# The start of a fused FFT and expert kernel: folds of a tile in one chain, classes of tiles by turns

## The chip, the cores and the metric

The kernel runs on one core of one Trainium2 chip. The time is device microseconds from launch to end; lower is better. Before the change three runs took 2414.26, 1863.13 and 1863.0 us, the median is 1863.13.

## The reference, cut to what matters

```python
batch, seq, dim = (8, 3008, 256)
X = np.fft.fft(x, axis=1)
X = np.fft.fft(X, axis=2)
x = X.real.astype(np.float32).reshape(B * S, D)     # (24064, 256)
h = x @ w_in                                         # w_in (256, 2048)
r = np.maximum(h, 0.0)
out = ((r * r) @ w_out).astype(np.float32)           # w_out (2048, 256)
```

The weights arrive as 64-bit floats, the activations as 32-bit ones.

## The kernel before, in words

The Fourier transform along the sequence is taken as products with cosine and sine tables, and its length is cut by symmetry before TensorE sees it. A batch is loaded as rows of four: n, -n, M-n and M+n (S is the length of the sequence, M half of it). A **fold** adds and subtracts these four and then the columns d and D-d. It leaves a tile `w` whose first 129 columns are for the cosine part, called P, and whose other 128 are for the sine part, called Q. The transform along the second axis is folded into the weights: a **window** of `w_in` is multiplied by cosine and sine matrices of size 256 (`dft_win`, L351), and the results are kept as G1 and G2 (`keep_win`). The **front** of a block is then G1 times P plus or minus G2 times Q, and relu and square follow; the **back** multiplies by `w_out`.

For batch 0 the rows are cut into seven tiles, by class: tile 0 (95 rows) and tile 1 (94 rows) of the classes 0 and 1, tiles 2 and 3 (96 and 92 rows) of class 2, called `TWO`, tiles 4 to 6 (128, 128 and 120 rows) of class 3, called `ODD0` onwards. Each class has its own cosine table; the sine table of tile 0 is loaded, the others are made by ScalarE from the cosine tables (`turn_table`, L228). A product group is named by its part and tile: P4 is the cosine product of tile 4, Q4 its sine product, E4 a small extra product for the sine part's lone column, which ScalarE scales out of `w` (L575) into `lone`. Each name stands for two products, for even and odd frequencies (`kp`). Products (L758) gather in PSUM; ScalarE copies the first quarter out (`copy`, L777), VectorE joins the groups step by step (`join_4`, `join_2`, `lo`; L799 to L811), and the odd group of each part is kept (`keep`, L818) for a later `rest` and `hi`.

The **head** is everything up to `sp` (`spread_e`, L983), which spreads the last row of Qt over all partitions, so that front half steps of block 0 (L999, L1001) can begin. The order of the head is written out by hand, and each engine takes its instructions in the order of the program. Six of seven tiles are folded in two halves on VectorE: the P half is `fs` (L554), `sc` (L563), `w` (L572, two steps), the Q half is `fd` (L559), `sc` (L567), `w` (two steps). Each step needs the one before it. The Q half of tile 5 is folded by GpSimd (`q_beside`, L1308 to L1312). All P halves but two come ahead of most Q halves. TensorE runs filler products on the identity matrix (`awake`, L255): 34 at the start, 5 before the first window, 2 before Q's joins; a filler is two matmul instructions in the trace, as is every product on 32-bit numbers.

Weights are converted from 64-bit to 32-bit numbers by a `round`: VectorE takes the signs (L300, phase TS), ScalarE scales the upper half and the lower half (L305 and L310, PU and PL), VectorE shifts and joins (L320, H), GpSimd adds the two (L329, PR). Windows 0 and 1 are begun in the head; the others, and the eight of `w_out`, run between the steps of block 0.

Loads go through SP's queue, those of the small tables through GpSimd's. Tiles 0 to 3 lie in the buffers that later hold `g`, tiles 4 to 6 and most raw weights in three buffers, and a raw weight's load waits until its buffer's last reader is done. For window 0 the last row of G2 is written to DRAM and read back by SP's queue as a column (`take_ends`); the windows named in `BY_PRODUCTS` get it by two products of one column (`ends_of`, L367) and a copy by VectorE (`keep_ends`, L371).

Behind the head stands `ORDER`, a list of tokens for block 0: `f0a` is TensorE's first half of front 0, `d0a` VectorE's half step for it (L1014 to L1017), `pgC1` and `pgD1` are the products of window 1 with the cosine and sine matrices, `GC1` and `GD1` keep them, `fe1` and `gE1` are its end products and their copy, `rl` and `sq` are relu and square, `bk` is a back step (L1122). After it comes the loop over all other blocks: L1028 is the front there, L1093 the back, on sums that GpSimd makes (L1056 to L1073).

Of the kernel before, what the change touches and what calls it, by code (L numbers as in the profile page):

```python
# [15 lines left out]
P = 128  # L16
# [68 lines left out]
def kernel(  # L85
# [84 lines left out]
    def load_x(b, t):  # L170
        if b and (t >= ODD0 or t == TWO + 1):
            xt[b, t] = xp.tile([P, 4, D], F32, name="xt", tag="x")
            for p, first, count, step in later_rows(t):
                nc.sync.dma_start(out=xt[b, t][p:p + count], in_=x[b, first:first + step * (count - 1) + 1:step])
            return
        c, r0, step, rows = TILES[t]

        while rows % 15 and rows % 16 and r0 + step * rows < NROW:
            rows += 1

        pool, tag = (gp, "g") if b == 0 and t < NT - NX else (xp, "x")
        xt[b, t] = pool.tile([P, 4, D], F32, name="xt", tag=tag)
        nc.sync.dma_start(out=xt[b, t][0:rows], in_=x[b, r0:r0 + step * (rows - 1) + 1:step])
# [68 lines left out]
    def awake(n):  # L252
        filled = psh.tile([P, CH], F32, name="filled", tag="h")
        for _ in range(n):
            nc.tensor.matmul(filled[:, 0:P], ident, ident, start=True, stop=True)  # L255
# [90 lines left out]
    def dft_win(j, side):  # L346

        tab, nm = ((cosd, "mC"), (sind, "mD"))[side]
        pg = psm.tile([P, CH], F32, name="pg", tag=nm) if j else psh.tile([P, CH], F32, name="pg", tag="h")
        for i in range(2):  # L350
            nc.tensor.matmul(pg, tab[:, i], win[j][:, i], start=i == 0, stop=i == 1)  # L351
        return pg

    BY_PRODUCTS = (1, 2)

    def keep_win(j, side, pg):
        to, v = (G1, G2)[side].rearrange("p (h j f) -> j p h f", h=2, j=NJ)[j], pg.rearrange("p (h f) -> p h f", h=2)
# [177 lines left out]
    def next_sums():  # L535
        nonlocal folds
        folds += 1
        return sums[folds % 2]

    def next_halves():  # L540
        nonlocal turns
        turns += 1
        return halved[turns % 2]

    def fold(t):


        r = slice(0, TILES[t][3])
        st = states[t] = {}
        folded[0, t] = w = wp.tile([P, 2, D + 1], F32, name="w", tag="w")  # L550

        def f_s():
            st["fs"], v = next_sums(), xt[0, t]
            tt(out=st["fs"][r, :, 0:D], in0=v[r, 0::2], in1=v[r, 1::2], op=ADD)  # L554

        def f_d():
            st["fd"] = fp.tile([P, 2, D], F32, name="fd", tag="fd")
            v = xt[0, t]
            tt(out=st["fd"][r], in0=v[r, 0::3], in1=v[r, 1:3], op=SUB)  # L559

        def f_sc():
            st["sc"], s = next_halves(), st["fs"]
            tt(out=st["sc"][r, :, PART[0]], in0=s[r, :, 0:H + 1], in1=s[r, :, D:H - 1:-1], op=ADD)  # L563

        def f_dc():
            st["sc"], d = next_halves(), st["fd"]
            tt(out=st["sc"][r, :, PART[1]], in0=d[r, :, 1:H + 1], in1=d[r, :, D - 1:H - 1:-1], op=SUB)  # L567

        def f_w(part):
            v = st["sc"]  # L570
            for kp in range(2):
                tt(out=w[r, kp, part], in0=v[r, 0, part], in1=v[r, 1, part], op=SUB if kp else ADD)  # L572

        def f_e():
            nc.scalar.mul(lone[r, 2 * t:2 * t + 2, P - 1:], w[r, :, H:H + 1], -0.5 if TILES[t][0] else 0.5)  # L575

        return [f_s, f_d, f_sc, f_dc, lambda: (f_w(PART[0]), f_e()), lambda: f_w(PART[1])]

    def by(i, a):
        return turn[0:HALF2, a, i:i + 1]  # L580
# [707 lines left out]

    pieces = [fold(t) for t in range(NT)]
    (_, start), *groups = dft_ops(0)
    groups = dict(groups)

    def for_p(t):
        for i in (0, 2, 4):
            pieces[t][i]()

    def for_q(t):
        for i in (1, 3, 5):  # L1300
            pieces[t][i]()

    def q_beside(t, behind):


        r, v = slice(0, TILES[t][3]), xt[0, t]
        gt, d = nc.gpsimd.tensor_tensor, states[behind]["sc"]
        gt(out=d[r, :, 0:D], in0=v[r, 0::3], in1=v[r, 1:3], op=ALU.subtract)  # L1308
        sc = next_halves()
        gt(out=sc[r, :, PART[1]], in0=d[r, :, 1:H + 1], in1=d[r, :, D - 1:H - 1:-1], op=ALU.subtract)  # L1310
        for kp in range(2):
            gt(out=folded[0, t][r, kp, PART[1]], in0=sc[r, 0, PART[1]], in1=sc[r, 1, PART[1]],  # L1312
               op=ALU.subtract if kp else ALU.add)

    def p_part(*names):
        for nm in names:
# [5 lines left out]
            for kp in range(2):  # L1322
                groups[1, kp, nm]()

    def folds_of(names):
        for nm in names.split():
            (for_p if nm[0] == "P" else for_q)(int(nm[1:]))

    def products_of(names):
        for nm in names.split():  # L1330
            (p_part if nm[0] == "P" else q_part)({"P": "", "Q": "", "E": "e"}[nm[0]] + nm[1:])

    start()
    awake(34)
    load_x(0, 0)
    load_x(0, 1)
    load_table(cosT, cos_s, (0,))
    nc.scalar.copy(turn[0:1, 0, 0:1], ident[0:1, 0:1])
    nc.gpsimd.tensor_copy(turn[0:1, 0, 1:2], xt[0, 0][0:1, 0, 0:1])
    load_table(cosT, cos_s, (1, TWO, TWO + 1), nc.gpsimd)  # L1340
    folds_of("P0 Q0 P1 Q1")
    raw = {("in", 0): load(pair_in(0))}
    first = round_win(0, raw["in", 0])
    first[0]()
    first[1]()
    load_x(0, 2)
    load_x(0, 3)
    for dst, src in ((cosd, cos_d), (sind[:, :, 0:P - 1], sin_d)):
        nc.sync.dma_start(out=dst, in_=src.rearrange("(c p) m -> p c m", p=P))
    load_table(sinT, sin_s, (0,), nc.gpsimd)  # L1350
    load_x(0, ODD0)
    load_x(0, ODD0 + 1)
    load_table(cosT, cos_s, (ODD0,))
    load_x(0, ODD0 + 2)
    load_table(cosT, cos_s, (ODD0 + 1, ODD0 + 2))
    for j in (1, 2):
        raw["in", j] = load(pair_in(j))
    folds_of("P2")
    first[2]()
    first[3]()  # L1360
    products_of("P0 E0 P1 E1")
    awake(5)
    for a in range(2):
        keep_win(0, a, dft_win(0, a))
    take_ends(0)
    folds_of("P3")
    products_of("P2 P3")
    p_part("copy")
    products_of("E2 E3")
    for t in range(1, ODD0):  # L1370
        turn_table(t)
    folds_of("P4 P5 Q2 P6 Q3 Q4")
    products_of("P4 Q0 Q1 E4 Q2 P5 P6")
    for t in range(ODD0, NT):
        turn_table(t)
    products_of("E5 Q3 E6 Q4")
    q_beside(5, 4)
    for nm in ("join_4", "join_2", "lo"):
        groups[0, 0, nm]()
    for nm in ("join_4", "join_2", "lo"):  # L1380
        groups[0, 1, nm]()
    p_part("keep")
    q_part("copy")
    products_of("Q5")
    second = round_win(1, raw["in", 1])
    second[0]()
    second[1]()
    folds_of("Q6")
    products_of("Q6")
    awake(2)  # L1390
    for nm in ("join_4", "join_2"):
        groups[1, 0, nm]()
    second[2]()
    second[3]()
    for nm in ("join_4", "join_2"):
        groups[1, 1, nm]()
# [48 lines left out]
    def piece_beside():  # L1445
# [7 lines left out]
    ROUNDED = ['3', 'w0', '4', 'w1', '5', 'w2', '6', 'w3', '7', 'w4', 'w5', 'w6', 'w7']  # L1453
    PHASES = ('TS', 'PW', 'H', 'PR', 'PU', 'PL')
    ORDER = (
# [8 lines left out]
    ).split()  # L1464
    rounds = {"2": round_win(2, raw["in", 2])}
    loaded, freed = [], set()
    made = {}

# [260 lines left out]
```

## Time and profile before

| | us |
|---|---|
| median of three runs | 1863.13 |
| the profiled execution | 1862.73 |
| its span, first to last instruction | 1860.9 |
| TensorE waits in the whole span, the seven kinds named added up | 4.4 |
| VectorE starts its first fold | 4.50 |
| TensorE starts its first product on data | 11.43 |
| the spread of Qt's last row (L983) | 34.13 |
| first back step of block 0 (L1122) | 47.76 |
| first front of the loop (L1028) | 91.42 |

The page gives busy times of each engine over the span. PE is TensorE's matmul, PEld its weight load, DVE is VectorE, ACT ScalarE, POOL GpSimd, SP the queue that issues most loads. Start times in a timeline are microseconds from the first instruction. An instruction's row ends with what ended the idle time ahead of it, where there was any. A row can hold several equal instructions (x2), and then its second number is the time from the first start to the last end. Two steps on VectorE that don't depend on each other overlap by some hundredths of a microsecond, so that the distance from start to start is a little shorter than the duration of a row.

### The profile page before, as it was taken

To read this page: it belongs to the slowest core of one execution; us is meant where nothing else is said; L and a number is where in the kernel's file an instruction comes from. 1 tells how busy PE (TensorE), PEld (TensorE's weight loads), DVE (VectorE), ACT (ScalarE), POOL (GpSimd) and SP (SyncE) were. 2 spreads that over 40 slices of the span, in tenths; PEclk is the share of its full clock that TensorE was granted. 3 is DMA by queue.
4 is the path that set the end of the run, shared out by engine and by line. 5 is a ranking of instruction groups with operands and counts; after the bars stand their busy time and mean duration, and the time that the engine had idled before them with its cause. 6 is when DMAs were issued, how large, how long until landed. Compare 5 with 4: busy or idle time off the path is not lost.

```text
span 1860.9 us, 33983 instructions
## 1 busy us (share of the span) xinstructions
PE 1852.5 (100%) x11368; PEld 1750.9 (94%) x11368; DVE 1475.5 (79%) x3483; ACT 1075.1 (58%) x1592; POOL 1461.7 (79%) x2137
## 2 busy tenths in 40 slices
PE   9999999999999999999999999999999999999999
PEld 7699999999999999999999999999999999999998
DVE  8998878887788878888788787888877887757666
ACT  4776646565556655666456565566645666444454
POOL 4499778788788887888778887788877878788885
PEclk9999999999999999999999999999999999999999
DMA  7441001110011111111011100111001100000010
GB/s 204 115 61 40 19 21 54 41 29 23 21 43 42 29 22 32 32 46 31 15 32 46 48 16 15 45 46 35 15 21 42 38 15 21 17 21 15 21 43 23
DMA packets 153541, 69.52 MB, mean 37 GB/s; under 512 B 132851, under 2 KB 144601, under 8 KB 153368
## 3 DMA queue, kind: packets, MB, share of 16 engines
q1 hardware_dynamic: 152822, 66.80, 14.5%
q8 instruction: 91, 1.49, 0.3%
q14 instruction: 82, 0.67, 0.1%
q0 software_dynamic: 416, 0.43, 0.1%
q10 hardware_dynamic: 130, 0.12, 0.0%
HBM read 42.60 MB, written 24.69 MB: 36 GB/s over the span
## 4 chain that ended last, share of the span: by engine, by line
PE 94%; DVE 3%; POOL 2%; ACT 1%; DMA 0%; issue 0%; SPq 0%; DVEq 0%; POOLq 0%; ACTq 0%
PE F L1093 34%; PE S L1093 23%; PE hQ L1028 17%; PE hP L1028 17%; PE pd L881 1%; PE pd L855 1%; PE pd L758 1%; DVE fd L320 1%; PE fin L1202 0%; DVE he L1014 0%; DVE w L572 0%; DVE wsum L404 0%; PE pg L351 0%; DVE g L1017 0%; DVE fs L554 0%
## 5 line engine op out<-in xcount | busy, mean ns | idle before, releaser
L1041 ACT ACTIVATE g<-g 128x1008 f32<-128x1008 f32 (+1 forms) x384 | 399.4, 1040 | 306.0 <-DVE g L1037 282.5
L1032 DVE SCALAR_TENSOR_TENSOR he<-ew,gE,hP 128x252 f32<-128x252 f32 (+1 forms) x748 | 321.3, 471 | 284.9 <-PE hP L1028 284.9
L1044 ACT ACTIVATE g<-g 128x1008 f32<-128x1008 f32 (+1 forms) x384 | 399.4, 1040 | 12.0
L1028 PE MATMUL hQ<-Qt,G 128*128 128x252 f32 (+3 forms) x1496 | 379.3, 376 | 0.6 <-ACT g L1041 0.5
L1028 PE MATMUL hP<-Pt,G 128*128 128x252 f32 (+1 forms) x1496 | 378.8, 376 | 0.0
L1093 PE MATMUL F<-s,wsum 128*128 128x168 f32 (+1 forms) x1496 | 335.4, 306 | 0.0
L1028 PEld LDWEIGHTS hQ<-Qt,G 128*128 128x128 f32 (+1 forms) x1496 | 281.6, 190 | 38.5 <-issue 2.6
L1093 PE MATMUL F<-g,wout 128*128 128x168 f32 (+1 forms) x1496 | 304.1, 305 | 0.0
L1066 POOL TENSOR_TENSOR s<-g 128x168 f32<-128x168 f32 (+1 forms) x187 | 100.8, 539 | 253.8 <-ACT g L1044 129.1
L1036 DVE TENSOR_TENSOR g<-he,hQ 128x504 f32<-128x504 f32 (+1 forms) x374 | 253.0, 676 | 41.0 <-DVE he L1032 1.8
L1028 PEld LDWEIGHTS hP<-Pt,G 128*128 128x128 f32 x1496 | 266.0, 190 | 18.7 <-issue 0.7
L1093 PE MATMUL S<-s,wout 128*128 128x168 f32 (+1 forms) x1496 | 280.6, 306 | 0.8 <-POOL s L1073 0.8
L1093 PE MATMUL F<-g,wsum 128*128 128x168 f32 (+1 forms) x1496 | 273.5, 305 | 0.0
L1093 PE MATMUL S<-s,wsum 128*128 128x168 f32 (+1 forms) x1496 | 273.5, 305 | 0.0
L1037 DVE TENSOR_TENSOR g<-he,hQ 128x504 f32<-128x504 f32 (+1 forms) x374 | 251.0, 671 | 0.0
L1093 PEld LDWEIGHTS F<-s,wsum 128*128 128x128 f32 x1496 | 247.6, 190 | 0.0
L1093 PEld LDWEIGHTS F<-g,wsum 128*128 128x128 f32 x1496 | 239.3, 190 | 8.1
L1093 PEld LDWEIGHTS S<-s,wsum 128*128 128x128 f32 x1496 | 239.3, 190 | 8.1
L1093 PEld LDWEIGHTS F<-g,wout 128*128 128x128 f32 x1496 | 239.4, 190 | 0.0
L1093 PEld LDWEIGHTS S<-s,wout 128*128 128x128 f32 x1496 | 231.0, 190 | 1.7 <-POOL s L1073 1.0
L1069 POOL TENSOR_TENSOR s<-s 128x336 f32<-128x336 f32 (+1 forms) x187 | 168.4, 901 | 14.7
L1072 POOL TENSOR_TENSOR s<-s 128x336 f32<-128x336 f32 (+1 forms) x187 | 167.7, 897 | 14.7
(221 smaller groups left out, 2484.3 us busy)
## 6 DMA issues: line engine op xcount, KB each, us to landing
out_dram<-os SPq DMA_DIRECT2D x376, 56.0 KB
xt<-in_x_dram SPq DMA_DIRECT2D x39, 384.0 KB
xt<-in_x_dram SPq DMA_DIRECT2D x63, 128.0 KB
raw<-in_moe_w_out_dram SPq DMA_DIRECT2D x20, 256.0 KB
ew<-e_dram SPq DMA_DIRECT2D x39, 126.0 KB
out_dram<-os SPq DMA_DIRECT2D x288, 7.0 KB
raw<-in_moe_w_in_dram SPq DMA_DIRECT2D x16, 256.0 KB
xt<-in_x_dram SPq DMA_DIRECT2D x2, 512.0 KB
```

The source lines that it names most:

```text
L320: nc.vector.scalar_tensor_tensor(out=e, in0=high, scalar=3, in1=e, op0=ALU.logical_shift_left, op1=ALU.bitwise_or)
L758: nc.tensor.matmul(ps[0:w.shape[-1]], w, part_of(cosT if lone_e else tab, t)[0:rows, kp, PLACE[t]:PLACE[t] + NC[kp][c]], start=t == ts[0] ...
L1028: nc.tensor.matmul(to[:, h, 0:n], w[:, fs], v[:, ks], start=h == 0, stop=True, skip_group_check=True)
L1032: nc.vector.scalar_tensor_tensor(out=t[:, h, 0:n], in0=window[b, k0][:, 0:n], scalar=gE[:, fc:fc + 1], in1=hP[:, h, 0:n], op0=ALU.mult, op ...
L1036: tt(out=g[:, :, 0:n], in0=t[:, :, 0:n], in1=hQ[:, :, 0:n], op=ALU.add)
L1037: tt(out=g[:, :, n:2 * n][:, :, ::-1], in0=t[:, :, 0:n], in1=hQ[:, :, 0:n], op=ALU.subtract)
L1041: act(g[:, :, 0:2 * n], g[:, :, 0:2 * n], AF.Relu)
L1044: act(g[:, :, 0:2 * n], g[:, :, 0:2 * n], AF.Square)
L1066: gt(out=s[:, 11], in0=b2[:, 0], in1=b1[:, 0], op=SUB)
L1069: gt(out=s[:, 4:6], in0=s[:, 4:6], in1=s[:, 10:11].to_broadcast([P, 2, tb]), op=SUB)
L1072: gt(out=s[:, 6:9:2], in0=s[:, 2:4], in1=s[:, 6:8], op=ADD)
L1093: nc.tensor.matmul(acc[nm][:, slot, 0:tb], w, v, start=q == 0 and nm not in begun, stop=q == end - 1, skip_group_check=True)
```

## The change

- A tile is folded in one go: both wide steps (sum and difference), both half steps, then `w` for P and Q together in two steps of 257 columns. GpSimd folds nothing.
- The tiles are taken by turns of the classes: 0, 4, 1, 5, 2, 3, 6. Each is followed by all its products P, E and Q. The loads and the tables stand in that order; tile 0's sine table is now the first load of GpSimd's queue, and window 0's raw block comes behind tile 2.
- Of the fillers 24 stand at the start and 7 behind P0 and E0; the others go.
- P's joins are set between the folds and the last products, Q's behind Q6. Window 0's products come between E6 and Q6, into another PSUM pool.
- Window 0's last row goes by end products and a copy in the head, no longer through DRAM.
- Window 1's step H (L320) and its GpSimd product move from the head to the start of `ORDER`, behind `sp`. In `ORDER` front half 0b moves ahead of window 1's products, and step H of window 2 goes behind `d0a`.

```diff
-    BY_PRODUCTS = (1, 2)
+    BY_PRODUCTS = (0, 1, 2)
...
+        fs, sc = next_sums(), next_halves()
+        fd = fp.tile([P, 2, D], F32, name="fd", tag="fd")
+        tt(out=fs[r, :, 0:D], in0=v[r, 0::2], in1=v[r, 1::2], op=ADD)
+        tt(out=fd[r], in0=v[r, 0::3], in1=v[r, 1:3], op=SUB)
+        tt(out=sc[r, :, PART[0]], in0=fs[r, :, 0:H + 1], in1=fs[r, :, D:H - 1:-1], op=ADD)
+        tt(out=sc[r, :, PART[1]], in0=fd[r, :, 1:H + 1], in1=fd[r, :, D - 1:H - 1:-1], op=SUB)
+        for kp in range(2):
+            tt(out=w[r, kp], in0=sc[r, 0], in1=sc[r, 1], op=SUB if kp else ADD)
...
     start()
-    awake(34)
+    awake(24)
...
+    fold(0)
+    products_of("P0 E0")
+    awake(7)
+    turn_table(ODD0)
+    fold(ODD0)
+    products_of("P4 E4 Q0")
+    products_of("Q4")
+    turn_table(1)
+    fold(1)
+    for j in (1, 2):
+        raw["in", j] = load(pair_in(j))
+    products_of("P1 E1 Q1")
+    p_part("copy")
+    turn_table(ODD0 + 1)
+    fold(ODD0 + 1)
+    p_part("join_4")
+    q_part("copy")
+    products_of("P5 E5 Q5")
     first[0]()
     first[1]()
...
+    turn_table(TWO)
+    fold(TWO)
+    products_of("P2 E2 Q2")
     first[2]()
     first[3]()
...
+    turn_table(TWO + 1)
+    fold(TWO + 1)
+    products_of("P3 E3 Q3")
+    turn_table(ODD0 + 2)
+    fold(ODD0 + 2)
+    products_of("P6 E6")
     second = round_win(1, raw["in", 1])
     second[0]()
     second[1]()
...
+    p_part("join_2")
+    for a in (1, 0):
+        keep_win(0, a, dft_win(0, a))
     products_of("Q6")
...
+    ends = ends_of(0)
+    q_part("join_4", "join_2")
+    p_part("lo", "keep")
+    keep_ends(0, ends)
     q_part("lo")
...
-        'sp TS2 PU2 f0a et PL2 TS3 H2 pgD1 PR2 d0a pgC1 f0b GC1 PW3 d0b pgC2 GD1 TSw0 rl0 fe1 f1b lc4 H3 PWw0 f1a gE1 PR3 '
+        'sp H1 PR1 TS2 PU2 TS3 f0a et PL2 f0b PW3 d0a H2 PR2 pgD1 d0b pgC1 GD1 TSw0 GC1 lc4 H3 PR3 rl0 PWw0 fe1 f1b gE1 pgC2 f1a '
```

More of the change, by code (lines that the diff above doesn't have):

```diff
@@ L348, in dft_win @@
         tab, nm = ((cosd, "mC"), (sind, "mD"))[side]
-        pg = psm.tile([P, CH], F32, name="pg", tag=nm) if j else psh.tile([P, CH], F32, name="pg", tag="h")
+        pg = psm.tile([P, CH], F32, name="pg", tag=nm) if j else psd.tile([P, CH], F32, name="pg", tag="d")
         for i in range(2):
@@ L545, in fold @@
     def fold(t):
-        r = slice(0, TILES[t][3])
-        st = states[t] = {}
+        r, v = slice(0, TILES[t][3]), xt[0, t]
         folded[0, t] = w = wp.tile([P, 2, D + 1], F32, name="w", tag="w")
[L552 to L577, printed above, removed]
+        fs, sc = next_sums(), next_halves()
[6 more added lines that the diff above has]
+            tt(out=w[r, kp], in0=sc[r, 0], in1=sc[r, 1], op=SUB if kp else ADD)
+        nc.scalar.mul(lone[r, 2 * t:2 * t + 2, P - 1:], w[r, :, H:H + 1], -0.5 if TILES[t][0] else 0.5)
     def by(i, a):
@@ L1287, in ahead @@
         return one + two
-    pieces = [fold(t) for t in range(NT)]
     (_, start), *groups = dft_ops(0)
     groups = dict(groups)
[L1295 to L1313, printed above, removed]
     def p_part(*names):
@@ L1323, in q_part @@
                 groups[1, kp, nm]()
-    def folds_of(names):
-        for nm in names.split():
-            (for_p if nm[0] == "P" else for_q)(int(nm[1:]))
     def products_of(names):
@@ L1333 @@
     start()
-    awake(34)
+    awake(24)
     load_x(0, 0)
+    load_table(cosT, cos_s, (0,))
+    load_x(0, ODD0)
     load_x(0, 1)
-    load_table(cosT, cos_s, (0,))
     nc.scalar.copy(turn[0:1, 0, 0:1], ident[0:1, 0:1])
     nc.gpsimd.tensor_copy(turn[0:1, 0, 1:2], xt[0, 0][0:1, 0, 0:1])
+    load_table(sinT, sin_s, (0,), nc.gpsimd)
     load_table(cosT, cos_s, (1, TWO, TWO + 1), nc.gpsimd)
-    folds_of("P0 Q0 P1 Q1")
+    load_table(cosT, cos_s, (ODD0,))
+    load_x(0, ODD0 + 1)
+    load_table(cosT, cos_s, (ODD0 + 1,))
@@ L1342 @@
+    load_x(0, TWO)
     raw = {("in", 0): load(pair_in(0))}
-    first = round_win(0, raw["in", 0])
+    load_x(0, TWO + 1)
+    for dst, src in ((cosd, cos_d), (sind[:, :, 0:P - 1], sin_d)):
+        nc.sync.dma_start(out=dst, in_=src.rearrange("(c p) m -> p c m", p=P))
+    load_x(0, ODD0 + 2)
+    load_table(cosT, cos_s, (ODD0 + 2,))
+    first = round_win(0, raw["in", 0])
+    fold(0)
[4 more added lines that the diff above has]
+    products_of("P4 E4 Q0")
@@ L1344 @@
+    products_of("Q4")
[10 more added lines that the diff above has]
+    products_of("P5 E5 Q5")
     first[0]()
     first[1]()
[L1346 to L1358, printed above, removed]
+    turn_table(TWO)
+    fold(TWO)
+    products_of("P2 E2 Q2")
     first[2]()
     first[3]()
[L1361 to L1383, printed above, removed]
@@ L1384 @@
-    products_of("Q5")
+    turn_table(TWO + 1)
[4 more added lines that the diff above has]
+    products_of("P6 E6")
     second = round_win(1, raw["in", 1])
@@ L1387 @@
     second[1]()
-    folds_of("Q6")
+    p_part("join_2")
+    for a in (1, 0):
+        keep_win(0, a, dft_win(0, a))
     products_of("Q6")
[L1390 to L1396, printed above, removed]
+    ends = ends_of(0)
+    q_part("join_4", "join_2")
+    p_part("lo", "keep")
+    keep_ends(0, ends)
     q_part("lo")
@@ L1464 @@
     ).split()
-    rounds = {"2": round_win(2, raw["in", 2])}
+    rounds = {"1": second, "2": round_win(2, raw["in", 2])}
     loaded, freed = [], set()
```

## The prediction, as put on record before the run

> **What bounds the kernel now.** I read the page's busy times first, then who waited for whom on TensorE, then the stages of the start in a table by stretches, then the timelines of TensorE, VectorE and GpSimd over the first 40 us.
>
> From the page, engine totals:
>
> ```profile
> PE 1852.5 (100%) x11368; PEld 1750.9 (94%) x11368; DVE 1475.5 (79%) x3483; ACT 1075.1 (58%) x1592; POOL 1461.7 (79%) x2137
> ```
>
> TensorE's waits over the whole span (two of seven rows; the longest is 1.4 us at the first instruction):
>
> ```profile
> PE pg L351 <- POOL win L329: 0.8, 1, 0.8
> PE S L1093 <- POOL s L1073: 0.8, 1, 0.8
> ```
>
> The stretches (length, then PE, PEld, DVE, ACT, POOL busy):
>
> ```profile
> 11.40:34.10 22.70, 21.73 (x108) 16.55 (x106) 21.80 (x63) 10.65 (x29) 6.85 (x8) 1.00 0.89 258
> 34.10:45.80 11.70, 11.38 (x54) 9.49 (x55) 9.31 (x25) 8.73 (x17) 3.68 (x3) 1.00 0.36 75
> 45.80:91.40 45.60, 45.60 (x153) 28.58 (x152) 42.61 (x92) 34.49 (x55) 19.69 (x16) 1.00 0.48 121
> ```
>
> TensorE has next to no hole after 45.8 us, so the end comes as much earlier as the dense stretch begins earlier. What matters is when the head ends: the spread of Qt's last row (L983) at 34.13. In the head the bound is VectorE: 21.80 busy of 22.70, and its row stretches from 4.50 to 34.07 without a wait. TensorE's rows there hold filler and products that start late:
>
> ```profile
> 1.37 10.22 PE L255 MATMUL filled<-ident 128*128 128x128 f32 x68 [1.37 <-POOL ident masks.py:199]
> 11.43 0.58 PE L758 MATMUL pd<-cosT,w 95*128 95x95 f32 x4
> 13.25 1.31 PE L255 MATMUL filled<-ident 128*128 128x128 f32 x10
> 19.77 1.43 PE L758 MATMUL pd<-cosT,w 128*128 128x377 f32 x4
> 33.34 0.61 PE L255 MATMUL filled<-ident 128*128 128x128 f32 x4
> 34.13 0.69 PE L983 MATMUL pe<-Qt,ident 128*128 128x252 f32 x2 [0.18 <-DVE Qt L737]
> ```
>
> VectorE, whose rows price a fold, and GpSimd beside it:
>
> ```profile
> 12.91 0.68 DVE L320 SCALAR_TENSOR_TENSOR fd<-raw,fd 128x512 uint32<-128x512 uint32 x1
> 13.52 0.68 DVE L554 TENSOR_TENSOR fs<-xt 92x512 f32<-92x512 f32 x1
> 14.23 1.37 DVE L563 TENSOR_TENSOR sc<-fs 92x258 f32<-92x258 f32 x1
> 16.77 0.43 DVE L563 TENSOR_TENSOR sc<-fs 128x258 f32<-128x258 f32 x1
> 17.23 0.49 DVE L572 TENSOR_TENSOR w<-sc 128x129 f32<-128x129 f32 x2
> 28.57 0.89 DVE L559 TENSOR_TENSOR fd<-xt 120x512 f32<-120x512 f32 x1
> 33.47 0.60 DVE L799 SCALAR_TENSOR_TENSOR Qt<-pd,signs,w 128x126 f32<-128x126 f32 x2
> 36.29 0.42 DVE L1016 TENSOR_TENSOR g<-he,ph 128x252 f32<-128x252 f32 x1
> ```
> ```profile
> 13.75 1.57 POOL L329 TENSOR_TENSOR win<-fd,m 128x512 int32<-128x512 int32 x1 [1.08 <-DVE fd L320]
> 25.82 1.30 POOL L1308 TENSOR_TENSOR sc<-xt 128x512 f32<-128x512 f32 x1 [10.50 <-DVE w L572]
> 36.15 1.27 POOL L329 TENSOR_TENSOR win<-fd,m 128x512 int32<-128x512 int32 x1 [2.40 <-ACT m L310]
> ```
>
> The sum of a tile took 1.37 us where 0.43 is usual, beside GpSimd's product of window 0. The step at 36.29 lies beside such a product too and is not lengthened; one of its inputs is in PSUM.
>
> **The folds.** A P half costs 1.59 us on VectorE (fs rows at 16.05 and 17.64), a Q half the same (24.07 to 25.66), each a chain in which every step waits for the one before. The new chain has its two wide steps side by side: 0.61 us each (12.91 to 13.52 is the spacing of two such rows without a dependence), 0.34 for the first half step (36.29 to 36.63 for the row's successor), 0.46 for the second up to its user (16.77 to 17.23), and twice 0.34 for w over all 257 columns in place of four steps: 2.7 us against 3.18. For seven tiles that is 18.9 us; before, 13 halves took 20.7 on VectorE, and the 14th 3.1 on GpSimd (25.82 to 28.92). VectorE so gains 1.8 us and takes back what GpSimd did.
>
> **The head, added up.** Tile 0 lands as before: VectorE starts at 4.50. Four folds (0, 4, 1, 5) end at 15.3. The order of loads follows them: by the DMA rates of the stretches (223 GB/s in the first 10 us, 285 in the next) the 0.99 MB up to tile 4 are through by about 6, the need is at 7.2; tile 5's 2.3 MB, with up to 0.4 MB of tables from GpSimd's queue, by 10.2 to 11.7, need 12.6. Nothing is charged; if tile 5 were 1 us late, 1 us is added. P's first joins then wait for TensorE: 24 fillers at 0.296 (10.05 us for 34) end at 8.5, P0 E0 take 0.9, 7 fillers at 0.26 end at 11.2; P4 E4 2.5 (0.63 a product of 377 columns), Q0 0.4, Q4 1.3, P1 E1 0.85: 16.2 with the copy of the first group under the second. So VectorE stands 0.9 us, and four joins at 0.16 end at 16.9. Window 0's raw block is now behind tile 2: 3.6 to 4.0 MB, that is 14.8 to 17.2; it is its L300 that waits, with the folds of 2, 3 and 6 queued behind it. I take no wait, since the joins end at 16.9; 0.3 is the bound. L300 0.35, fold 2 to 19.95, L320 to 20.55. GpSimd's product of window 0 now falls beside fold 3, as it fell beside the step at 14.23: I charge 0.95, that row's excess (bounds 0 and 1.57, the whole product). Fold 3 ends at 24.2, and fold 6's first w is there at 26.65. Tile 6 and its table, 5.2 to 5.5 MB in all, are through by 20.5 to 22.5 (210 GB/s from 20 on), window 1's raw block by 24.5, each 2 us or more ahead of its user; the cover gone, each us late is one us.
>
> From here TensorE leads: P6 E6 2.5, window 0 (L351) 1.7, Q6 1.3, the new end products of window 0 0.4 (the row at 43.64 up to the next, 44.01): 32.5. VectorE has its L300 (0.35), P's joins (four at 0.27, rows 26.10 and 26.37), Q's (2.4, 30.44 to 33.47 less one L320) and P lo (0.4) done at 31.1, so they are covered with 1.3 us to spare. Then the copy into gE with its wait 0.3, Qt's two joins 0.6, spread at 33.4: **0.7 us earlier** than 34.13.
>
> **What is moved past the head.** Window 1's L320 (0.61) and its GpSimd product (1.27) now come behind the spread; VectorE's two L300 and the first half step of block 0 queue behind that L320. Ahead of L351 of window 1 TensorE has the spread 0.43 and now both halves of front 0, 1.7. The product is ready 0.05 before the spread plus 0.69, 1.27 and up to 0.42 for an L300 in its way: 2.0 to 2.4 against 2.1. I charge 0.3. In 34.1 to 45.8 VectorE idles 2.4 us, which hides the 0.61; without that idle it would be 0.61. The write and read of window 0's last row through DRAM go: they held SP's queue, so raw blocks 3, w0, 4 and w1 start earlier; by the table DMA has room (75 GB/s), a gain I count at nothing, as none of VectorE's waits names a raw block. ScalarE has the same table turns, spread out; it is busy 10.65 of 22.70.
>
> Sum: 0.7 less 0.3, that is 0.4 earlier. The profiled execution took 1862.73 (span 1860.9), so 1862.3; the median of the runs is 0.4 above it: **1862.7**.
>
> [...]
>
> **The rivals.**
> *The cover holds:* no step is held beside GpSimd, and window 1 comes in time: 0.95 and 0.3 more, 1861.4. For it: a new fold has its wide steps back to back, and GpSimd may find its place between. Against: the row at 14.23. 0.2.
> *GpSimd holds VectorE behind the spread (slower):* L300 and L320 have only SBUF inputs, and two windows' products come there at once. Such rows cost 1.77 and 2.01 in place of 0.69 at 55.16 and 57.20 beside GpSimd's 55.08 and 57.08, that is 1.1 and 1.3 more. If both hit before TensorE is dense, block 0's half steps and the next windows come 2.4 later and no hole later on gives it back: 1862.7 + 2.4 = 1865.1. It decides when the holds exceed the 2.4 us that VectorE idles there, or fall on the two window products. [...] No row shows two windows at the spread: 0.25.
> *It leads nowhere:* the head ends earlier, but raw blocks or GpSimd's sums (100.0 busy of 108.6 in 91.4 to 200) set the next stage: 1863.1. Against: both follow from the same head, and TensorE waited on them 0.8 us once. 0.1.
>
> **How the numbers follow.** Forecast 0.45, rivals 0.2, 0.25, 0.1. Downwards the cover's 1861.4 less the 0.9 of P's joins, if TensorE comes sooner, is 1860.5; upwards 1865.1, with the 1 us of a late tile 1866.1. Leaving out under a tenth at each end: 1860.8 to 1865.8. A measurement of this kernel tells about 2% from no change, 37 us; the whole head is 34 us and no case reaches it: within 2% 0.97, faster 0.01, slower 0.02.
>
> **What would show it.** Folds of 2.7 us; one VectorE step of fold 3 lengthened beside window 0's product; P6 behind 26.6; the spread near 33.4; L351 of window 1 waiting no more than 0.4 for GpSimd; L1028's first row, 91.42 before, near 91.0. Wrong if VectorE waits for a load between 4.5 and 27, if Q6's products start after 31.5, or if TensorE's holes between the spread and the first plain product (L1122) grow.

## The result, and the profile after

Twenty runs of the kernel after took 1866.64 us in the median (1863.32 to 1869.21), beside 1863.05 for the kernel before on the same chip (all but one run of it between 1862.71 and 1863.96): ratio 1.0018, 95% interval 1.0011 to 1.0024. The forecast was 1862.7, its range ended at 1865.8. The kernel became slower by 3.6 us, and its time, which hardly moved before, now scatters over 6 us. The profiled execution took 1864.92 (span 1863.1, before 1860.9), 2.2 more than the profiled one of before but 1.7 less than the median.

The page's totals of the kernel after:

```profile
PE 1852.8 (99%) x11352; PEld 1749.8 (94%) x11352; DVE 1475.5 (79%) x3474; ACT 1074.8 (58%) x1592; POOL 1458.6 (78%) x2133
```

The same three stretches as before. Columns: length, busy time of PE, PEld, DVE, ACT, POOL with instruction counts, granted TensorE clock, DMA share, GB/s:

```profile
11.40:34.10 22.70, 20.71 (x85) 14.84 (x85) 19.30 (x50) 9.26 (x27) 2.77 (x3) 0.92 1.01 269
34.10:45.80 11.70, 10.79 (x54) 8.85 (x53) 10.49 (x27) 8.03 (x17) 3.87 (x3) 1.00 0.24 46
45.80:91.40 45.60, 45.60 (x157) 29.31 (x156) 42.56 (x93) 34.51 (x57) 20.50 (x15) 1.00 0.48 123
```

Two columns of the first row matter. VectorE is busy 19.30 of 22.70 where it was busy 21.80, 2.5 us less, in part because Qt's joins and window 1's L320 now lie behind 34.1; it stands idle for 3.4 us. The granted clock is 0.92 where it was 1.00.

TensorE's timeline. The lines of the program have moved: L739 is a product, L964 the spread:

```profile
8.99 0.58 PE L739 MATMUL pd<-cosT,w 95*128 95x95 f32 x4
11.45 1.43 PE L739 MATMUL pd<-cosT,w 128*128 128x377 f32 x4
22.41 0.80 PE L739 MATMUL pd<-sinT,w 96*127 96x189 f32 x4
25.14 0.92 PE L739 MATMUL pd<-cosTl,w 92*128 92x189 f32 x4 [1.92 <-DVE w L557]
27.90 2.43 PE L739 MATMUL pd<-cosTl,w 120*128 120x377 f32 x4
30.16 1.43 PE L739 MATMUL pd<-cosTl,wsum 120*128 120x377 f32 x4
33.16 1.43 PE L739 MATMUL pd<-sinTl,w 120*127 120x377 f32 x4
35.78 0.66 PE L964 MATMUL pe<-Qt,ident 128*128 128x252 f32 x2 [0.86 <-DVE Qt L718]
```

Products start at 8.99 in place of 11.43, but the spread comes at 35.78 in place of 34.13. TensorE stands 1.92 us ahead of P3 until fold 3's `w` is there. P6, at 27.90, takes 2.43 us; E6 behind it, of the same shape, takes 1.43. The clock tells why. The same columns, in three stretches of 3.41 us laid on the step of the granted clock:

```profile
23.00:26.41 3.41, 1.49 (x10) 1.24 (x9) 3.38 (x7) 0.34 (x2) 0.40 (x1) 1.00 1.09 290
26.41:29.82 3.41, 3.41 (x9) 2.37 (x8) 3.38 (x12) 2.50 (x5) 0.00 (x0) 0.50 1.05 381
29.82:33.23 3.41, 3.41 (x15) 2.53 (x14) 2.22 (x9) 0.38 (x1) 0.00 (x0) 1.00 0.84 266
```

Behind the stretch in which TensorE worked 1.49 of 3.41 us the granted clock was 0.50 for one stretch of that length, and then 1.00 again.

VectorE's timeline, where the folds' lateness comes from (L552 to L557 are the steps of a fold, L300 and L320 those of a raw block):

```profile
7.96 0.69 DVE L552 TENSOR_TENSOR fs<-xt 128x512 f32<-128x512 f32 x1 [0.88 <-DMA xt<-in_x_dram]
16.44 0.25 DVE L786 TENSOR_TENSOR db<-da,pd 128x95 f32<-128x95 f32 x1 [0.37 <-ACT da L758]
17.98 0.43 DVE L300 TENSOR_SCALAR fd<-raw 128x512 uint32<-128x512 uint32 x1 [0.80 <-DMA raw<-in_moe_w_in_dram]
22.20 1.75 DVE L553 TENSOR_TENSOR fd<-xt 92x512 f32<-92x512 f32 x1
25.34 0.68 DVE L552 TENSOR_TENSOR fs<-xt 120x512 f32<-120x512 f32 x1
34.97 0.16 DVE L371 COPY gE<-pe 128x2 f32<-128x2 f32 x1 [2.93 <-PE pe L367]
36.17 1.84 DVE L300 TENSOR_SCALAR fd<-raw 128x512 uint32<-128x512 uint32 x2
```

GpSimd, whose products lie beside the lengthened rows at 22.20 and 36.17:

```profile
21.84 1.56 POOL L329 TENSOR_TENSOR win<-fd,m 128x512 int32<-128x512 int32 x1 [8.87 <-DVE fd L320]
36.40 1.33 POOL L329 TENSOR_TENSOR win<-fd,m 128x512 int32<-128x512 int32 x1 [13.00 <-DVE fd L320]
```

VectorE waits for tile 4 of x (0.88), for P's copy (0.37) and for window 0's raw block (0.80), and one wide step of fold 3 takes 1.75 in place of 0.68; fold 6 starts at 25.34. Behind the spread nothing is lost: the first back step is at 49.23, 13.45 us behind the spread, where it was 13.63. In the loop another 0.6 us is added in this execution: the first fronts stand 1.50 behind those of before, the ones from 739 us on 2.13.

### The profile page after: what moved, and what is told of

Its sections match the earlier page's. It is cut to its first block, busy times and chain, and to the rows that moved or that the text cites. A ratio compares the mean times of both kernels' runs of the same rounds, so it can differ in the third digit from the quotient of the medians.

```text
span 1863.1 us, 33926 instructions
## 1 busy us (share of the span) xinstructions
PE 1852.8 (99%) x11352; PEld 1749.8 (94%) x11352; DVE 1475.5 (79%) x3474; ACT 1074.8 (58%) x1592; POOL 1458.6 (78%) x2133
## 3 DMA queue, kind: packets, MB, share of 16 engines
q8 instruction: 91, 1.49, 0.3%
## 4 chain that ended last, share of the span: by engine, by line
PE 94%; DVE 2%; POOL 1%; ACT 0%; issue 0%; DMA 0%; SPq 0%; DVEq 0%; POOLq 0%; ACTq 0%
PE F L1074 34%; PE S L1074 23%; PE hQ L1009 17%; PE hP L1009 17%; PE pd L862 1%; PE pd L836 1%; PE pd L739 1%; DVE fd L320 0%; PE pg L351 0%; PE fin L1183 0%; DVE he L995 0%; DVE wsum L404 0%; DVE g L998 0%; DVE g L997 0%; PE ph L982 0%
```

## The experiments

Two theories. **C (clock):** TensorE's holes ahead of the late tiles put it at half clock (0.50 in the row at 26.41), each time for 3.41 us, in which it loses about half of that; how often it happens differs between executions, hence the scatter. **L (lateness):** loads that come late and the GpSimd product beside fold 3 make the fold chain itself later, and the clock is a side issue. The runs were made on three chips; each is set against the kernel before on the same chip (33 runs, 1863.0 to 1863.41 in the median).

| kernel | median, us | over before | ratio, 95% interval | range of 11 runs |
|---|---|---|---|---|
| after, again | 1867.22 | +4.2 | 1.0018, 1.0010 to 1.0027 | 1865.07 to 1868.33 |
| after, fillers in the holes | 1865.16 | +2.2 | 1.0011, 1.0002 to 1.0020 | 1863.52 to 1868.28 |
| after, late product | 1863.72 | +0.7 | 1.0003, 0.9994 to 1.0012 | 1862.76 to 1865.61 |
| after, no fillers behind P0 | 1867.36 | +4.4 | 1.0021, 1.0012 to 1.0030 | 1865.20 to 1868.40 |
| before, without the five fillers | 1864.07 | +0.7 | 1.0004, 0.9995 to 1.0013 | 1862.81 to 1865.92 |
| after, loads | 1864.59 | +1.2 | 1.0008, 0.9999 to 1.0017 | 1864.23 to 1865.58 |
| after, window 1 back | 1867.13 | +3.7 | 1.0017, 1.0008 to 1.0026 | 1865.08 to 1867.67 |
| after, tail alone | 1866.12 | +3.0 | 1.0015, 1.0006 to 1.0023 | 1863.96 to 1867.24 |
| after, loads and late product | 1861.72 | -1.4 | 0.9992, 0.9983 to 1.0001 | 1861.38 to 1862.12 |
| **all three combined** | 1860.66 | -2.8 | 0.9987, 0.9978 to 0.9995 | 1859.84 to 1863.22 |
| combined, ends behind the spread | 1860.86 | -2.2 | 0.9987, 0.9978 to 0.9996 | 1859.78 to 1862.98 |
| before, three of five fillers | 1863.67 | +0.6 | 1.0002, 0.9993 to 1.0011 | 1862.61 to 1864.61 |

### The kernel after once more

> The changed kernel once more, unaltered. Theory C (clock): TensorE stands idle 1.9 us ahead of P3, and the granted clock then goes to half for one or more stretches of 3.4 us, in P3 to Q6; the profile shows such a stretch, its length or place not the same as in the first profile, and the times scatter over 1863 to 1869. Theory L (lateness): what is lost is lost to loads and to the GpSimd product beside fold 3 (spread 1.1 us later than worked out); the half clock is a by-product, and the times lie close to the first profile's 1864.9.

The excess is there again, on another chip. The eleven times fall into two groups, five of 1865.07 to 1865.70 at a mean clock of 0.999 and six of 1867.22 to 1868.33 at 0.998. A stretch of 3.41 us at half clock takes 0.0009 off the mean over 1863 us, so the groups would fit one and two such stretches. The mean can't prove it: it also takes in half clock behind TensorE's last product (0.50 from 1860.00 us to the end of the kernel before, where TensorE runs nothing), and the kernel before without its five fillers, further on, shows 0.998 with one stretch in its head. The profiled execution is of the first group: a hole of 2.15 us ahead of P3, one stretch of half clock (0.50 from 26.96 to 30.37 us). None of the second group was profiled.

### Fillers in the holes

```diff
     products_of("P2 E2 Q2")
+    fill(7)
...
     products_of("P3 E3 Q3")
+    fill(2)
```

The fillers are products on the identity into unused columns of the PSUM bank in which P's odd group gathers. With them the output is off from the reference by a relative 0.116, which is put down here to that group's sums; no step of VectorE, ScalarE or GpSimd is touched.

> Seven filler products after Q2 and two after Q3, into columns of a PSUM bank that nothing reads; all else as in the changed kernel. C: granted clock 1.00 in every stretch, P6 E6 back at 2.5 us, the spread near 34.5 instead of 35.8, times 1863.4 with a scatter under 1 us. L: the folds come no earlier, so the median stays at 1866 and the scatter stays.

In the profile the holes and the half clock are gone: the granted clock is 1.00 from 22 to 36 us, P6 takes 1.53 in place of 2.43, and the spread is at 34.64:

```profile
27.65 1.53 PE L745 MATMUL pd<-cosTl,w 120*128 120x377 f32 x4
34.64 0.66 PE L972 MATMUL pe<-Qt,ident 128*128 128x252 f32 x2 [0.86 <-DVE Qt L724]
```

The median falls by 2.06 against the kernel after on the same chip, without a fold moved. That is theory C's part. But 2.2 us over before stay, and the clock isn't all of that, nor all of the scatter: nine of the eleven executions have a mean clock of 1.000, which leaves no room for a stretch at half clock (one would give 0.999), and they lie between 1863.52 and 1866.21, at 1864.45 in the median. Something else varies too. This run doesn't tell what, as its profiled execution is the second fastest of the eleven, 1.4 below their median.

### The GpSimd product behind the last fold

```diff
-    first[2]()
-    first[3]()
     turn_table(TWO + 1)
     fold(TWO + 1)
     products_of("P3 E3 Q3")
     turn_table(ODD0 + 2)
     fold(ODD0 + 2)
+    first[2]()
+    first[3]()
```

> Window 0's L320 and its GpSimd product go from behind fold 2 to behind fold 6; no filler is added. Fold 3's lengthened step (1.75) goes back to 0.68 and L320's 0.61 leaves the chain, so fold 6's w comes 1.7 us earlier and the hole ahead of P3 shrinks from 1.9 to 0.3. C: clock 1.00, the spread near 33.0, 1862.2 with little scatter. L: 1866.6 less 1.7, that is 1864.9, with the scatter unchanged.

TensorE's timeline in that kernel:

```profile
21.84 0.92 PE L739 MATMUL pd<-cosT,w 96*128 96x189 f32 x4 [0.87 <-DVE w L557]
24.51 0.92 PE L739 MATMUL pd<-cosTl,w 92*128 92x189 f32 x4 [0.47 <-DVE w L557]
27.18 1.53 PE L739 MATMUL pd<-cosTl,w 120*128 120x377 f32 x4 [0.47 <-DVE w L557]
34.17 0.66 PE L964 MATMUL pe<-Qt,ident 128*128 128x252 f32 x2 [0.86 <-DVE Qt L718]
```

One hole of 1.9 us has become three of 0.87, 0.47 and 0.47, and no half clock shows in the head: the rows next behind these three take 0.80, 0.80 and 1.43, as Q2 and E6 did in the kernel after at a granted clock of 1.00. The spread is back at 34.17, though VectorE here waited 1.94 us for the raw block, longer than in the kernel after. One product moved, which both takes the hold off fold 3 and spreads the hole, is worth 3.5 us of the median (1867.22 to 1863.72, the same chip). It can't tell the two theories apart; the fillers above and the hole in the kernel before, further on, can. Seven of its eleven executions have a mean clock of 1.000 and still lie between 1862.90 and 1865.61.

### More hole: no fillers behind P0

```diff
     products_of("P0 E0")
-    awake(7)
```

> The seven fillers behind P0 and E0 are left out, which opens a second hole of 1.6 us ahead of P4, where TensorE has 1.9 us to spare. C: in some executions half clock from about 11 us on as well; where it does, TensorE reaches P3 later and with no hole there, so the time is anything from 1863.5 to 1868, and the profile shows which. L: no change from the changed kernel, since no fold waits for these products except P's joins.

Median and range are those of the kernel after, as theory L expected; theory C allowed them too, so the times decide nothing here. The hole came, not where it was opened (0.42 us ahead of P4) but further on, 1.55 ahead of P2 and 1.77 ahead of P3, as the products ran ahead of the folds. Five stretches of 3.41 us (the columns as above):

```profile
20.32:23.73 3.41, 1.86 (x11) 1.63 (x11) 3.38 (x8) 2.29 (x7) 0.62 (x1) 1.00 1.04 249
23.74:27.15 3.41, 1.64 (x6) 1.14 (x5) 3.38 (x6) 0.43 (x2) 0.93 (x1) 0.50 1.09 308
27.15:30.56 3.41, 3.41 (x12) 3.41 (x12) 3.38 (x11) 1.81 (x5) 0.00 (x0) 0.50 1.06 382
30.56:33.97 3.41, 3.41 (x6) 1.80 (x6) 2.82 (x11) 0.50 (x1) 0.00 (x0) 0.50 0.74 224
33.97:37.38 3.41, 3.41 (x15) 2.48 (x14) 0.00 (x0) 1.16 (x4) 0.00 (x0) 1.00 0.33 2
```

The first two stretches, with a hole each, are followed by half clock. So is the third (27.15), in which TensorE was busy throughout, at half clock. The spread is at 39.03.

### The clock alone: a hole in the kernel before

```diff
     products_of("P0 E0 P1 E1")
-    awake(5)
```

> The kernel before with its filler products awake(5) between the products of tiles 0 and 1 and those of window 0 left out; nothing else is changed. TensorE then stands still from 13.2 to 15.4 us, where it ran fillers, and no engine has a step that starts later for it. If the holes of TensorE lower its granted clock and the fold chain has no part in this (theory C): a stretch at half clock of 3.41 us behind the hole, the products in it twice as long, the spread 0.9 to 1.7 us behind 34.13, and 0.9 to 1.7 us on the time, 1864.0 to 1864.8, with a scatter as in the kernel after. If only the lateness of the folds counts (theory L): the clock stays at 1.00 and the time at 1863.0.

TensorE's timeline in that kernel:

```profile
15.22 1.13 PE L351 MATMUL pg<-win,cosd 128*128 128x256 f32 x4 [1.84 <-POOL win L329]
17.44 1.46 PE L758 MATMUL pd<-cosT,w 96*128 96x189 f32 x4
18.69 1.46 PE L758 MATMUL pd<-cosTl,w 92*128 92x189 f32 x4
35.47 0.69 PE L983 MATMUL pe<-Qt,ident 128*128 128x252 f32 x2
```

The same rows in the kernel before with its fillers (its spread is at 34.13):

```profile
15.37 1.13 PE L351 MATMUL pg<-win,cosd 128*128 128x256 f32 x4 [0.81 <-POOL win L329]
17.20 0.80 PE L758 MATMUL pd<-cosT,w 96*128 96x189 f32 x4
17.84 0.80 PE L758 MATMUL pd<-cosTl,w 92*128 92x189 f32 x4
```

The stretches without the fillers:

```profile
13.24:16.65 3.41, 1.57 (x9) 1.28 (x8) 3.31 (x7) 0.26 (x1) 1.56 (x1) 1.00 1.02 309
16.65:20.06 3.41, 3.41 (x12) 3.22 (x11) 3.20 (x9) 0.83 (x4) 0.00 (x0) 0.50 1.05 250
```

The fillers compute nothing, and no product starts later for want of them: window 0 comes at 15.22, before at 15.37. Still the first rows of P2 and P3 take 1.46 where they took 0.80, and the spread is at 35.47 in place of 34.13. All of the loop stands 1.3 us later, and so does the span, 1862.2 beside 1860.9. So in this execution the hole cost 1.3 us by the clock alone; theory L expected none of this. The median moved by 0.7 only, less than the 0.9 to 1.7 expected, and its interval holds 1: two of eleven runs (1862.81 and 1863.07, mean clock 1.000) show no loss.

### The loads alone

```diff
     load_x(0, 0)
-    load_table(cosT, cos_s, (0,))
     load_x(0, ODD0)
+    load_table(cosT, cos_s, (0,))
...
-    first[0]()
-    first[1]()
     turn_table(TWO)
     fold(TWO)
+    first[0]()
+    first[1]()
     products_of("P2 E2 Q2")
     first[2]()
     first[3]()
```

> The kernel after with tile 4 of x loaded ahead of the cosine rows of tile 0, and the first step of window 0's raw block moved behind the fold of tile 2; the GpSimd product stays where it was. By theory L the wait of 0.88 us for tile 4 and that of 0.80 for the raw block go, the folds end about 1.2 us earlier (fold 6's first w at about 26.6), and the spread comes at about 34.6 at full clock; GpSimd's product still costs its 1.07 us beside a fold. By theory C the hole ahead of the third tile's products stays (the product beside the fold makes it), so that the half clock stays in part of the executions: median 1864.5 to 1866. If both holes close: 1863.3 to 1864.

Tile 4 and the raw block are no longer waited for, but the folds hardly gain: fold 6 starts at 25.03 in place of 25.34, not 1.2 earlier. P's joins now wait 1.03 us for the copy (0.37 before the edit), and L320, directly behind L300, waits 0.73 for ScalarE. Fold 3's step again takes 1.75 beside the product, the hole ahead of P3 is 2.08, and the half clock stays, one stretch (Q3 takes 1.46 and P6 2.40, E6 behind them 1.43). Theory L's size for the folds was wrong here; C's range for the median holds.

```profile
24.83 0.92 PE L739 MATMUL pd<-cosTl,w 92*128 92x189 f32 x4 [2.08 <-DVE w L557]
```
```profile
25.03 0.68 DVE L552 TENSOR_TENSOR fs<-xt 120x512 f32<-120x512 f32 x1
```

Yet the edit did more than this execution shows. It gains 0.3 on the profiled execution of the kernel after (1864.59 beside 1864.92), but the median is 1.2 over before, where the kernel after stood 3.6 and 4.2 over it, and the eleven times lie within 1.4 us. It seems that nearly every execution has one stretch, and that the slower executions of the kernel after lost more to loads than its profiled one did. Both are argued: only one execution was profiled.

### Window 1 back in the head

```diff
-    q_part("join_4", "join_2")
+    for nm in ("join_4", "join_2"):
+        groups[1, 0, nm]()
+    second[2]()
+    second[3]()
+    for nm in ("join_4", "join_2"):
+        groups[1, 1, nm]()
...
-        'sp H1 PR1 TS2 ...
+        'sp TS2 ...
...
-    rounds = {"1": second, "2": round_win(2, raw["in", 2])}
+    rounds = {"2": round_win(2, raw["in", 2])}
```

> The kernel after with the second step and the GpSimd product of window 1 back between Q's joins, as before the change, and not behind the spread. The prediction charged the move with 0.3 us. By what the trace of after shows (spread to first back step 13.45 us against 13.63) it cost nothing: the time is then that of the kernel after, 1866.6 to 1867.3, or up to 0.7 us over it, as the second step lies ahead of the spread again. If the move was what cost (rival): 1863 to 1864.

No gain: the move was not what cost. The first back step comes 13.4 us behind the spread (38.00 to 51.39), as with the move (13.45). Its profiled execution had two stretches of half clock, the second behind one in which TensorE was busy 3.33 of 3.41:

```profile
25.70:29.11 3.41, 3.33 (x11) 3.33 (x12) 3.38 (x10) 1.42 (x5) 0.00 (x0) 0.50 1.05 381
29.11:32.52 3.41, 3.41 (x8) 2.25 (x7) 3.34 (x12) 1.32 (x2) 0.45 (x1) 0.50 0.88 281
```

### Loads, late product and tail together

```diff
     load_x(0, 0)
-    load_table(cosT, cos_s, (0,))
     load_x(0, ODD0)
+    load_table(cosT, cos_s, (0,))
...
     load_x(0, TWO)
-    raw = {("in", 0): load(pair_in(0))}
     load_x(0, TWO + 1)
-    for dst, src in ((cosd, cos_d), (sind[:, :, 0:P - 1], sin_d)):
-        nc.sync.dma_start(out=dst, in_=src.rearrange("(c p) m -> p c m", p=P))
     load_x(0, ODD0 + 2)
+    raw = {("in", 0): load(pair_in(0))}
     load_table(cosT, cos_s, (ODD0 + 2,))
+    for dst, src in ((cosd, cos_d), (sind[:, :, 0:P - 1], sin_d)):
+        nc.sync.dma_start(out=dst, in_=src.rearrange("(c p) m -> p c m", p=P))
...
     fold(TWO + 1)
+    first[0]()
+    first[1]()
     products_of("P3 E3 Q3")
     turn_table(ODD0 + 2)
     fold(ODD0 + 2)
+    first[2]()
+    first[3]()
...
     p_part("join_2")
+    products_of("Q6")
     for a in (1, 0):
         keep_win(0, a, dft_win(0, a))
-    products_of("Q6")
     ends = ends_of(0)
     q_part("join_4", "join_2")
     p_part("lo", "keep")
-    keep_ends(0, ends)
     q_part("lo")
+    keep_ends(0, ends)
```

The four calls of `first` are taken out of their old places between fold 5 and fold 3.

> The kernel after with the loads in the order in which the folds need them (tile 4 of x second, tile 3 and 6 ahead of the raw block and of the window's tables), window 0's raw step behind the fold of tile 3 and its second step and GpSimd product behind the fold of tile 6, Q6's products ahead of window 0's, and the copy of gE behind Q's last join. By both theories together nothing is left that made the kernel after slower: VectorE waits for no load between 4.5 us and the folds' end but for tile 6 (which landed at 23.3), TensorE has no hole over 1 us ahead of its products, the spread comes at 30.5 to 32.5, the clock is 1.00, and the time is 1859.5 to 1861.5, under both kernels. If instead the loads set the pace (16 queues that are already busy), the folds move no earlier and the time is that of the run with the late product, 1863.7.

TensorE's and VectorE's timelines in that kernel:

```profile
24.73 1.53 PE L739 MATMUL pd<-cosTl,w 120*128 120x377 f32 x4 [0.29 <-DVE w L557]
27.37 1.43 PE L739 MATMUL pd<-sinTl,w 120*127 120x377 f32 x4
31.00 0.69 PE L964 MATMUL pe<-Qt,ident 128*128 128x252 f32 x2
```
```profile
7.30 0.68 DVE L552 TENSOR_TENSOR fs<-xt 128x512 f32<-128x512 f32 x1
15.92 0.25 DVE L786 TENSOR_TENSOR db<-da,pd 128x95 f32<-128x95 f32 x1 [0.52 <-ACT da L758]
19.85 0.68 DVE L553 TENSOR_TENSOR fd<-xt 92x512 f32<-92x512 f32 x1
24.25 0.76 DVE L557 TENSOR_TENSOR w<-sc 120x257 f32<-120x257 f32 x2
30.90 0.16 DVE L371 COPY gE<-pe 128x2 f32<-128x2 f32 x1 [0.82 <-PE pe L367]
```

No wait for a load, fold 3's step at 0.68, one hole of 0.29, a granted clock of 1.00 from 11.40 to 45.80 us, the spread at 31.00: 3.1 us ahead of the kernel before, of which 2.7 reach the end of the span. This kernel beats both, ratio 0.9987 (0.9978 to 0.9995).

### Which part of the combination

The combined kernel with the tail of the kernel after:

> The combined kernel with its tail as in the kernel after: window 0's products ahead of Q6's, the copy of gE ahead of Q's last join. Loads in the order of the folds and the late GpSimd product stay. If the loads and the hold beside the fold were the lateness (theory L, with C's half clock gone because the holes are gone), P6 stays at 24.7 us, the spread comes 1.3 us behind the combined kernel's 31.0, at 32.3, and the time is 1861.5 to 1862.3. If the tail was most of the gain (rival): 1863 or more.

Spread at 32.53, time 1861.72: loads and late product without the tail already turn +4 into -1.4, with the smallest scatter of all, 0.7 us, though its interval still holds 1. The tail on its own, in the kernel after:

> The kernel after with only its tail changed: Q6's products ahead of window 0's, the copy of gE behind Q's last join; loads, raw steps and the GpSimd product as they were. The hole ahead of the fourth row tile's products stays, and so does the half clock in most executions. Expected: the spread 1.3 us earlier than in the kernel after, at 34.5 in an execution with one stretch of half clock, and the time 1865.2 to 1866.0. If the tail was most of the gain: 1864 or less.

A hole of 2.14 ahead of P3, one stretch of half clock (Q3 1.47, P6 1.83, E6 1.43), the spread at 35.10, 0.7 earlier than in the kernel after and not 1.3, as the folds were no earlier and VectorE was late for the spread by 0.25. The time is 0.1 above what was expected. Little is gained from the tail as long as the holes are there.

Window 0's end products behind the spread (`fe0` and `gE0` become tokens of `ORDER`):

> The combined kernel with window 0's four products of one column (ends, 0.5 us) and the copy of gE moved from ahead of the spread to behind it. If TensorE's order is what bounds the spread there, it comes at 30.4 to 30.6 and the time falls by 0.2 to 0.5 us at most, as the products are still made behind it; if nothing is gained, the front behind the spread is bound by VectorE: 1860.7 as before.

Nothing gained. Its profiled execution, at a mean clock of 1.000, has a span 2.0 us longer than that of the combined kernel: P's joins waited 1.44 us for the copy (0.52 there) and L300 0.95 for the raw block (not at all there), so that P6 came at 26.60 in place of 24.73, behind a hole of 1.16. With the loads of the combined kernel, too, the raw block came late, here by 0.95; why the copy did was not followed up.

### A shorter hole in the kernel before

> The kernel before with awake(3) in place of awake(5): a hole of about 1.3 us ahead of window 0, between the holes that brought half clock so far (1.55 to 2.08 us in one period of 3.41 us) and those that did not (up to 0.87). Theory C says only that it lies between: half clock for 3.41 us and a time near 1864.1 in some executions or none. Theory L: 1863.0 to 1863.4 and full clock in all.

Inconclusive. In the profiled execution P0 started 0.31 later than before and P1 waited 0.30 us for its table, and the fillers ran that much later, so that the hole was 0.60 and not 1.3. The mean clock was 1.000, and P2 and P3 took 0.80 as in the kernel before; behind the other holes of 0.87 us and less no half clock came either.

## Why the prediction was wrong

**What was right.** Folds take 2.7 us (7.96 to 10.64). The hold of fold 3 beside GpSimd's product is 1.07 (1.75 less 0.68), charged with 0.95. From the start of fold 6 to the spread the prediction had 9.2 us (24.2 to 33.4); without the half clock, worked out below, it took 0.1 more. TensorE is dense behind 45.8 as before. The hold is on the step at 22.20, whose inputs are both parts of xt, and 1.20 us of the product's 1.56 lay behind the start of that step.

**The step that failed first: "Nothing is charged" for the loads, and "I take no wait" for the raw block.** Tile 4 was put at 6 by a mean rate of bytes; it landed at 7.94 and cost 0.88. The raw block, "14.8 to 17.2", landed at 17.89 and cost 0.80, over the bound of 0.3. Against this stand 0.53 less wait at P's joins (0.37, not 0.9) and a start 0.18 sooner; with the hold 0.12 over, fold 6 starts 1.1 later than worked out: at 25.34 in place of 24.2. The working of the loads doesn't come out of its rates either: at 223 GB/s, then 285, 0.99 MB are through at 4.4 us and 4.0 MB at 16.2, where it wrote about 6 and 17.2, and even these were too early. A mean rate didn't give the landing of a single tile here; the order did, as the run with the loads moved shows: with tile 4 ahead of tile 0's cosine rows its wait is gone.

**The step that was missing: TensorE's granted clock.** The sum took the products at their full-clock durations in all places, and counted fillers that go at nothing. The holes that open between products that run ahead and folds that don't were in the sum, as TensorE's waits, but only for their own length. In the profiled execution P6 took 1.0 us more by the half clock (2.43 beside E6's 1.43), and it started up to 0.15 late, as P3's last rows, at half clock too, held TensorE until 27.90; all of this lies on the path. Waits and hold 1.1, clock 1.15 and 0.1 of the tail are the 2.4 by which the spread misses 33.4. Behind the spread 0.5 came back (0.18 gained where 0.3 was charged); 0.6 was added in the loop. So 1862.3 became 1864.9 in this execution, to within 0.1. At the first of the two added places in the loop, at 581 us, a front waits 0.25 for a fold step of VectorE (L618); what the rest is was not followed up.

**From this execution to the median** it is 1.7 us more, of which the forecast had 0.4; here the cause stays open. The two groups 2 us apart with mean clocks of 0.999 and 0.998, and an execution with two stretches (the kernel with window 1 back, 1867.18), would fit one to two stretches in the typical execution. But at a mean clock of 1.000 the kernel with fillers still spreads over 2.7 us, and another order of loads brought the median from 3.6 and 4.2 over before down to 1.2 while the half clock stayed in the profiled execution. So late loads have a part in it that the profiled execution of the kernel after doesn't show. Beyond the 2.06 us that the fillers took off the median, how much is clock and how much is loads is not known, since executions at the upper end were not profiled.

**What the traces show of the clock.** The granted clock shows two levels, 0.50 and 1.00, and the stretches at 0.50 that were read in the head are 3.41 us long (26.41 to 29.82 in the kernel after), 6.82 (25.70 to 32.52, window 1 back) and 10.23 (23.74 to 33.97, no fillers behind P0). A stretch began anywhere from 0.08 us ahead of a hole's end (25.70, the hole up to 25.78, window 1 back) to 1.68 behind it (23.74 and 22.06, no fillers behind P0). In the stretches of 3.41 us ahead of the half clock TensorE stood for 1.55 us (1.86 busy, no fillers behind P0), 1.84 (1.57 busy, the kernel before without its five), 1.92 (1.49 busy, the kernel after) and 2.09 (1.32 busy, the kernel after once more).

**The rivals.** "GpSimd holds VectorE behind the spread" priced the profiled execution about right, 1865.1, by luck: the hold came (two L300 together took 1.84 there, about 1.1 more than usual), but VectorE's idle time took it up, and moving window 1 back gained nothing. "Leads nowhere" falls as well: the next stage follows the head one to one, by +1.5 and, in the combined kernel, by -3.1. "The cover holds" needed fold 3 unheld; the combined kernel has that and goes below its 1861.4, with other changes besides.

**Its tests.** Folds, the lengthened step and L351 of window 1 (no wait at all) came out as written. P6 was behind 26.6, at 27.90, and the loop's first front came at 92.9, not near 91.0. What would make it wrong did: VectorE waited for loads between 4.5 and 27, and Q6's products started at 33.16, not before 31.5. The third sign did not: behind the spread nothing was lost. One sum was off by 0.1 (0.69, 1.27 and up to 0.42 less 0.05 are 1.9 to 2.3, not 2.0 to 2.4), with no effect.

## What to carry to other kernels

Fillers that compute nothing carried the clock here: from 16.65 to 20.06 us the kernel before was granted 1.00 with its five and 0.50 without. Before taking such fillers out, add up the idle time that TensorE is left with, and price a hole like those here (1.55 to 2.15 us) not at its length alone but at another 1.0 to 1.3 us for the products behind it, in most executions here and not in all. When one engine is made faster or started sooner, ask which engine it now waits for, give that one its loads first, and set the GpSimd step that holds it behind its own chain; here the same folds lost 4 us or won 1.4 by the order of loads and the place of one GpSimd product, and won 3 with the tail changed too. A new scatter is a hint to look at the clock of each execution, and at the loads: at a mean clock of 1.000, too, the times here lay up to 2.7 us apart, and one profiled execution explains itself and not the median.

## What was unexpected of the hardware

- In the head, a hole of 1.55 to 2.15 us was followed by half clock in seven profiled executions of six kernels, for 3.41, 6.82 or 10.23 us where the clock was read by stretches; holes of 0.87 us and less were not. Nor was one of 1.16 (the combined kernel with the ends behind the spread, where the two rows behind the hole take 1.53 and 1.43). What decides between 1.16 and 1.55 us was not shown.
- Half clock went on for another 3.41 us though TensorE was busy nearly throughout the stretch before (3.41 of 3.41 us at 27.15 in the kernel without fillers behind P0, 3.33 of 3.41 at 25.70 in the one with window 1 back). In the kernel after, and in the kernel before without its five fillers, the clock was 1.00 again after one stretch (29.82 to 33.23, 20.06 to 23.47). What makes the difference stays open.
- The same load came 1.04 us later in one execution than in another: window 0's raw block let L300 start at 17.98 in the kernel after and at 19.02 in the one with the late product, whose loads up to there are the same.
